# First tokens, first key weights and first key chunks of a gated attention and MLP block, loaded and multiplied in other halves

## The chip, the cores and the metric

The kernel runs on one core of one Trainium2 chip. Its metric is the device time of one execution in microseconds (us), of which several runs are taken and the median is given. The core has a matrix engine (PE, with its weight loads listed as PEld), a vector engine (DVE), an activation engine (ACT), a general engine (POOL) and a synchronising engine (SP), which here issues all DMA transfers. Each engine works through its own list of instructions in order and waits on semaphores for the others.

## The reference

`x` is 2048 tokens of 512 features. Two branches are computed from it and mixed by a gate for each token:

```
g   = sigmoid(sum(x * gate_w))                  # one number for each token
a   = attention(x) @ wo                         # 32 heads of 16, four segments of 512 tokens
b   = (gelu(x @ w_gate) * (x @ w_up)) @ w_down  # 512 -> 1792 -> 512
out = g * a + (1 - g) * b
```

In each segment the attention is causal softmax attention over that segment's 512 tokens. To it is added, by a share for each head, `sigmoid(beta)`, the reading of a memory of the segments before: with phi(t) = t+1 for t>0 and exp(t) otherwise, the memory M sums phi(k) v and z sums phi(k), and the reading is phi(q) M / (phi(q) z). All data is bfloat16, sums are in float32.

## The kernel before, in words

The segments are worked through in order, s = 0 to 3. For a segment, x is kept transposed in `xS[s % 3]`, as 128 features x 4 feature chunks x 512 tokens, so that it can be either operand of a matmul. Keys and queries are made in four chunks of 128 features (eight heads): `u_k(s, c)` (line 364) and `u_q(s, c)` (line 278) each run four matmuls of 128x512 over the feature chunks `fc` into one bank of PSUM, and then `cast` (line 298) copies the bank to bfloat16. For keys two further DVE instructions (line 378) write the chunk twice, with alternate heads zeroed, into `KTm`, which has room for NK = 3 chunks. Values (`u_v`, line 393) take four tiles of 128 tokens.

All these results share one pool, `pgen`, of four PSUM banks, which are handed out in turn by `gen(name)` (line 125). A tile that gets a bank has to wait until the earlier tile in that bank has been read out.

The first stretch is written out by hand; afterwards a planner in Python sets the order of the work from costs and due times. The hand-written part is:

- `load_inputs` (line 134): SP issues, one after the other, two transfers for the first 512 tokens of x, two for wk, then wq, gate_w, wv, beta and w_gate. The two halves of x have 256 tokens each, and partition p gets the two neighbouring tokens 2p and 2p+1 of the half, 2 KB in one piece. The halves of wk are halves of its columns: 256 of the 512 output features, for all input features, in pieces of 512 bytes.
- `warm_up` (line 161): matmuls on constants, whose results are not used.
- `transpose_x0` (line 175): PE transposes these tokens, in four groups of four blocks of 128x128 (token half, and pair of feature chunks). Each group has a bank, which DVE copies to `xS[0]` for the feature chunks 0 and 1, and ACT for 2 and 3. As neighbouring tokens lie in two different blocks, the copies write with a step of two elements.
- `u_k(0, c)` for c = 0, 1, 2 (line 769), `u_q(0, c)` for four chunks, `load_rest` (line 149, further DMA issues), a small transpose of gate_w, four value tiles, the remaining values (`u_vz`), the issue of copies of V, and 14 gate tiles (`u_gate`), which ACT reads out directly.

In this stretch all casts of keys, queries and values go to DVE, since `limit[0]` is still zero. The banks in turn are: warm-up 0 and 1; the four transposed groups 2, 3, 0, 1; key chunks 0 to 2 in 2, 3, 0; query chunks 0 to 3 in 1, 2, 3, 0; gate_w in 1; value tiles 0 to 3 in 2, 3, 0, 1; `u_vz` in 2. So value tile 0 waits for the cast of query chunk 1.

Of the kernel before, what the change touches and what calls it, by code (L numbers as in the profile page):

```python
# [11 lines left out]
ALU = mybir.AluOpType  # L12

P = 128
D = 512
# [4 lines left out]
FC = D // P  # L20
NC8 = H // 8
# [3 lines left out]
NK = 3  # L25
NX = 3
NB = 8
# [9 lines left out]
MM512 = 0.216  # L37
# [16 lines left out]
def kernel(  # L54
# [15 lines left out]
    nc = tc.nc  # L70
# [4 lines left out]
    x2 = A_x[0]  # L75
# [8 lines left out]
    def const(shape, dtype, name):  # L84
        return cpool.tile(shape, dtype, name=name, tag=name)

    xS = [const([P, FC, L], BF, f"x{i}") for i in range(NX)]
    wq = const([P, FC, D], BF, "wq")
    wk = const([P, FC, D], BF, "wk")
# [7 lines left out]
    eo = const([P, 2], F32, "eo")  # L97
# [7 lines left out]
    ktb = const([P, NC8, L], BF, "ktb")  # L105
# [4 lines left out]
    KTm = const([P, NK, NB, 2, 64], BF, "KTm")  # L110
# [14 lines left out]
    def gen(name):  # L125
        return pgen.tile([P, 512], F32, name=name, tag="gen")
# [4 lines left out]
    def cols(dst, src):  # L131
        nc.sync.dma_start(dst[:, :, :], src.rearrange("(fc p) n -> p fc n", p=P))

    def load_inputs():
        half = L // 2
        for i in range(2):
            nc.sync.dma_start(x0[:, 2 * i:2 * i + 2, :],
                              x2[half * i:half * (i + 1), :].rearrange("(p k) d -> p k d", p=P))
        for i in range(2):
            n = slice(D // 2 * i, D // 2 * (i + 1))  # L140
            cols(wk[:, :, n], A_wk[:, n])
        cols(wq, A_wq)
        nc.sync.dma_start(gw4, gate_w.rearrange("(fc p) -> fc p", p=P))
        cols(wv[:, :, 0:D], A_wv)
        nc.sync.dma_start(beta[:, :], A_beta.rearrange("(o n) -> o n", o=1).to_broadcast((P, H)))
        for n in (slice(0, 4 * P), slice(4 * P, DFF)):
            cols(wga[:, :, n], B_w_gate[:, n])
# [27 lines left out]
    def transpose_x0():  # L175
        for half in range(2):
            for f0 in range(0, FC, 2):
                T = pgen.tile([P, 1024], BF, name="x0T", tag="gen")
                for i in range(4):
                    fc, k = f0 + i // 2, i % 2  # L180
                    nc.tensor.transpose(T[:, i * P:(i + 1) * P],
                                        x0[:, 2 * half + k, fc * P:(fc + 1) * P], ident[:, :])
                dst = xS[0][:, f0:f0 + 2, half * 256:half * 256 + 256].rearrange(
                    "q f (p k) -> q f k p", k=2)
                src = T[:, 0:512].rearrange("q (f k p) -> q f k p", f=2, k=2)
                if f0 == 0:
                    nc.vector.tensor_copy(dst, src)
                else:
                    nc.scalar.copy(dst, src)
# [105 lines left out]
    def near(end):  # L295
        return t_act[0] - 1.0 <= end and max(t_act[0], end) + CAST_T <= limit[0]

    def cast(out, src, scale=1.0):
        end = t_pe[0] + MM512
        if near(end):  # L300
            nc.scalar.activation(out, src, AF.Copy, scale=scale)
            t_act[0] = max(t_act[0], end) + CAST_T
            spared[0] = EVAC
        elif isinstance(scale, float):
            nc.vector.tensor_copy(out, src)  # L305
        else:
            nc.vector.tensor_scalar_mul(out, src, scale)
# [7 lines left out]
    general_now = [False]  # L315
# [43 lines left out]
    def u_phk(s, c):  # L359
        def f():  # L360
            phi(ktb[:, c:c + 2, :], ktb[:, c:c + 2, :], ("k", s, c), 1)
        return 0.0, 0.0, f

    def u_k(s, c):
        def f():
            T = gen("kT")
            for fc in range(FC):
                nc.tensor.matmul(T[:, :], lhsT=wk[:, fc, c * P:(c + 1) * P],  # L368
                                 rhs=xS[s % NX][:, fc, :],
                                 start=(fc == 0), stop=(fc == FC - 1))  # L370
                if fc < FC - 1:
                    yield MM512
            cast(ktb[:, c, :], T[:, :])
            if general_now[0]:
                return MM512
            for p in range(2):
                eng = nc.vector if s == 0 and c < NK else nc.gpsimd
                eng.tensor_scalar(out=KTm[:, (NC8 * s + c) % NK, :, p, :],  # L378
                                  in0=ktb[:, c, :].rearrange("q (b k) -> q b k", b=NB),
                                  scalar1=eo[:, p:p + 1], scalar2=None, op0=ALU.mult)  # L380
            return MM512
        return 4 * MM512, EVAC, f

    pk_at = {}

# [226 lines left out]
    def group_qk(pieces):  # L612
        lg = plg.tile([P, 4, 512], F32, name="lg", tag="lg")
        for i, b, off in pieces:
            n = L - 64 * b
            for j in range(4):
                rows = slice(32 * j, 32 * j + 32)
                nc.tensor.matmul(lg[:, j, off:off + n],  # L618
                                 lhsT=KTm[rows, i % NK, b].rearrange("r p k -> r (p k)"),
                                 rhs=QT[rows, i % NC8, 64 * b:L],  # L620
                                 start=True, stop=True, tile_position=(32 * j, 0))
        pT = ptp.tile([P, 4, 512], BF, name="pT", tag="pT")
        nc.scalar.activation(pT[:, :, :], lg[:, :, :], AF.Exp, scale=DH ** -0.5)  # L623
        for _, b, off in pieces:
            for r in range(2):
                v = pT[64 * r:64 * r + 64, :, off:off + 64]
                nc.gpsimd.affine_select(out=v, in_=v, pattern=[[0, 4], [1, 64]],  # L627
                                        compare_op=ALU.is_ge, fill=0.0, base=0,
                                        channel_multiplier=-1)
        return pT  # L630
# [35 lines left out]

    ctx.enter_context(tc.manual_schedule())
    load_inputs()
    make_identity(nc, ident[:, :])
    warm_up()  # L670
    transpose_x0()
    setup_consts()

# [88 lines left out]
    def run(u):  # L762
        if u[0] == 0.0:
            u[2]()
        else:
            for _ in u[2]():
                pass

    for c in range(NK):
        run(u_k(0, c))  # L770
    for c in range(NC8):
        run(u_q(0, c))
    load_rest()
# [34 lines left out]
    for i in range(NK, NSEG * NC8):  # L808
        s, c = i // NC8, i % NC8
        us.append(unit(u_k(s, c), first(i) - 12, ("k", s),  # L810
                       lambda i=i, s=s, c=c: clock[0] >= last(i - NK) and
                       (s == 0 or count(("pk", s - 1)) > c)))
        if c % 2 == 1 and s < NSEG - 1:
            us.append(unit(u_phk(s, c - 1), 0, None,
                           lambda s=s: s == 0 or count(("pk", s - 1)) == NC8))
    streams.append(Stream("K", us))
    us = []
    for i in range(NC8, NSEG * NC8):
        s, c = i // NC8, i % NC8
# [140 lines left out]
    for pieces in visits:  # L960
        clock[0] += 1
        for i, b, off in pieces:
            s, c = i // NC8, i % NC8
# [4 lines left out]
        s = pieces[0][0] // NC8  # L968
        t = group_qk(pieces)
# [8 lines left out]
        if lumps and lumps[0][0] == clock[0]:  # L978
            i = lumps.pop(0)[1]
# [5 lines left out]
        n = len(visits) - clock[0]  # L985
# [80 lines left out]
    def general():  # L1066
# [3 lines left out]
        for s in range(NSEG):  # L1070
# [4 lines left out]
            for c in range(NC8):  # L1075
                run(u_k(s, c))
                run(u_q(s, c))
# [40 lines left out]
            if s < NSEG - 1:  # L1118
# [4 lines left out]
                for half in range(2):  # L1123
# [3 lines left out]
                            scalar1=float(DH ** 0.5 * D * D), scalar2=EXP_LIMIT,  # L1127
                            op0=ALU.mult, op1=ALU.is_le)
# [31 lines left out]
```

## Time and profile before

| what | us |
|---|---|
| median of the runs (lowest, highest) | 270.71 (270.58, 271.08) |
| the profiled execution | 270.57 |
| its span, first to last instruction | 268.8 |
| PE busy in the span | 262.3 |
| ACT busy | 209.0 |
| DVE busy | 203.7 |
| POOL busy | 156.8 |
| first matmul of the keys starts (from the start of the span) | 5.83 |
| first matmul of the queries | 8.50 |
| first matmul of the values | 12.17 |
| first matmul of the gate | 15.69 |

The profile lists instructions with their line in the kernel, engine, tile and duration, and the idle time of the engine ahead of them with what ended it. Matmuls overlap in the records: one of 128x512 is listed with 380 ns, but they start every 216 ns. DVE's records overlap in the same way: the casts of 0.68 us start every 0.60 us. "DMA" as a releaser means that an engine waited for a transfer to land. Times in the profile are from the start of the span, and 1.8 us of the execution lie outside it.

### The profile page before, as it was taken

The numbers are of one execution on the slowest core, as the hardware profiler recorded it, in microseconds if no ns is written. First come the engines' busy times: TensorE is split into PE (matmuls) and PEld (weight loads), VectorE is DVE, ScalarE is ACT, GpSimd is POOL, SyncE is SP. The second block draws the span as 40 slices with busy tenths as digits, with TensorE's granted clock in tenths as the row PEclk, the third lists the DMA queues.
The fourth block names the chain that finished last, engine by engine and source line by source line (L and its number), as shares of the span: only waits on it lengthen the run. The fifth ranks groups of instructions, "written<-read, shape, count | busy, mean of one in ns | idle before, by whom it ended". The sixth has DMA issues, their size and how long they took to land.

```text
span 268.8 us, 6576 instructions
## 1 busy us (share of the span) xinstructions
PE 262.3 (98%) x2713; PEld 117.5 (44%) x2713; DVE 203.7 (76%) x390; ACT 209.0 (78%) x163; POOL 156.8 (58%) x298
## 2 busy tenths in 40 slices
PE   7999999999999999999999999999999999999993
PEld 3454434344453444445444444444444544344441
DVE  2999575868777887697986979596898588697374
ACT  3237889999997998889999988889888987567420
POOL 4000168897905979987811998596875089654400
PEclk9999999999999999999999999999999999999998
DMA  6999901200160000301052002110000200001102
GB/s 205 334 211 321 331 18 35 41 4 0 29 136 2 0 22 22 78 4 41 0 68 56 2 21 50 33 34 8 20 24 21 66 2 20 19 3 41 39 22 85
DMA packets 30282, 16.60 MB, mean 62 GB/s; under 512 B 20008, under 2 KB 28968, under 8 KB 30248
## 3 DMA queue, kind: packets, MB, share of 16 engines
q1 hardware_dynamic: 30248, 16.14, 22.9%
q8 instruction: 22, 0.36, 0.6%
q14 instruction: 12, 0.10, 0.1%
HBM read 8.14 MB, written 2.10 MB: 38 GB/s over the span
## 4 chain that ended last, share of the span: by engine, by line
PE 86%; POOL 5%; issue 4%; DMA 2%; ACT 1%; SPq 0%; DVE 0%; ACTq 0%; DVEq 0%; POOLq 0%
PE gT L456 19%; PE uT L477 17%; PE dT L493 14%; PE lg L618 8%; PE od L643 6%; PE aT L510 5%; PE qT L282 5%; PE kT L368 5%; PE vT L397 4%; POOL pT L627 3%; POOL KTm L378 2%; DMA wk<-in_A_wk_dram 2%; PE MT L531 1%; PE mn L600 1%; ACT pT L623 1%
## 5 line engine op out<-in xcount | busy, mean ns | idle before, releaser
L627 POOL TENSOR_SCALAR_AFFINE_SELECT pT<-pT 64x256 bf16<-64x256 bf16 x256 | 113.8, 445 | 94.2 <-ACT pT L623 81.4
L623 ACT ACTIVATE pT<-lg 128x2048 bf16<-128x2048 f32 x72 | 135.1, 1876 | 24.9 <-PE lg L618 21.6
L477 PE MATMUL uT<-x,wup 128*128 128x512 bf16 x224 | 60.4, 380 | 0.0
L456 PE MATMUL gT<-x,wga 128*128 128x512 bf16 x224 | 57.0, 380 | 0.0
L493 PE MATMUL dT<-wdn,G 128*128 128x512 bf16 x224 | 52.9, 380 | 0.0
L483 DVE TENSOR_TENSOR G<-uT,G 128x512 bf16<-128x512 f32 x56 | 38.1, 684 | 6.4 <-PE uT L477 6.2
L378 POOL TENSOR_SCALAR KTm<-ktb,eo 128x512 bf16<-128x512 bf16 x26 | 40.6, 1572 | 1.3
L650 DVE STREAM_TRANSPOSE oq<-od 128x512 f32<-128x512 f32 x32 | 21.0, 695 | 19.5 <-PE od L643 19.5
L493 PEld LDWEIGHTS <-G 128*128 128x128 bf16 x224 | 20.8, 98 | 25.0 <-issue 2.1
L456 PEld LDWEIGHTS <-wga 128*128 128x128 bf16 x224 | 20.5, 98 | 23.9 <-issue 2.2
L477 PEld LDWEIGHTS <-wup 128*128 128x128 bf16 x224 | 19.8, 97 | 24.0 <-issue 5.4
L618 PE MATMUL lg<-QT,KTm 32*128 32x192 bf16 (+7 forms) x512 | 28.5, 287 | 0.0
L305 DVE CAST G<-gT 128x512 bf16<-128x512 f32 x24 | 16.5, 688 | 9.7 <-PE gT L456 9.5
L618 PEld LDWEIGHTS <-KTm 32*128 32x128 bf16 x512 | 8.3, 92 | 28.4 <-issue 28.1
L643 PE MATMUL od<-pT,V 64*32 64x128 bf16 (+7 forms) x512 | 19.4, 284 | 0.2 <-POOL pT L627 0.2
L643 PE MATMUL od<-pT,Vs 64*32 64x128 bf16 (+7 forms) x512 | 19.4, 284 | 0.0
L471 ACT ACTIVATE G<-G 128x3584 bf16<-128x3584 bf16 x6 | 18.8, 3182 | 0.0
L656 DVE SCALAR_TENSOR_TENSOR o<-oq,ogs,rden 128x256 bf16<-128x256 f32 x32 | 17.0, 532 | 1.1
L368 PE MATMUL kT<-x,wk 128*128 128x512 bf16 x64 | 16.8, 380 | 0.9 <-DMA wk<-in_A_wk_dram 0.9
L282 PE MATMUL qT<-x,wq 128*128 128x512 bf16 x64 | 16.6, 379 | 0.0
L515 DVE SCALAR_TENSOR_TENSOR tB<-aT,gct,tB 128x512 bf16<-128x512 f32 x16 | 11.9, 746 | 6.0 <-PE aT L510 5.7
L510 PE MATMUL aT<-wo,oT 128*128 128x512 bf16 x64 | 16.5, 380 | 0.0
(96 smaller groups left out, 274.8 us busy)
## 6 DMA issues: line engine op xcount, KB each, us to landing
out_dram<-tB SPq DMA_DIRECT2D x16, 128.0 KB, 1.7
wup<-in_B_w_up_dram SPq DMA_DIRECT2D x1, 1792.0 KB, 8.4
wdn<-in_B_w_down_dram SPq DMA_DIRECT2D x1, 1792.0 KB
wga<-in_B_w_gate_dram SPq DMA_DIRECT2D x1, 1280.0 KB, 10.2
Vs<-V SPq DMA_DIRECT2D x8, 144.0 KB, 2.6
G<-in_A_x_dram SPq DMA_DIRECT2D x2, 256.0 KB, 2.8
wk<-in_A_wk_dram SPq DMA_DIRECT2D x2, 256.0 KB, 4.2
wq<-in_A_wq_dram SPq DMA_DIRECT2D x1, 512.0 KB, 5.7
```

The costliest lines, as they stand in the source:

```text
L282: nc.tensor.matmul(T[:, :], lhsT=wq[:, fc, c * P:(c + 1) * P], rhs=xS[s % NX][:, fc, :], start=(fc == 0), stop=(fc == FC - 1))
L368: nc.tensor.matmul(T[:, :], lhsT=wk[:, fc, c * P:(c + 1) * P], rhs=xS[s % NX][:, fc, :], start=(fc == 0), stop=(fc == FC - 1))
L378: eng.tensor_scalar(out=KTm[:, (NC8 * s + c) % NK, :, p, :], in0=ktb[:, c, :].rearrange("q (b k) -> q b k", b=NB), scalar1=eo[:, p:p + 1], ...
L456: nc.tensor.matmul(T[:, :], lhsT=wga[:, fc, hs * P:(hs + 1) * P], rhs=xS[s % NX][:, fc, :], start=(fc == 0), stop=(fc == FC - 1))
L477: nc.tensor.matmul(T[:, :], lhsT=wup[:, fc, hs * P:(hs + 1) * P], rhs=xS[s % NX][:, fc, :], start=(fc == 0), stop=(fc == FC - 1))
L483: nc.vector.tensor_tensor(out=g, in0=T[:, :], in1=g, op=ALU.mult)
L493: nc.tensor.matmul(T[:, :], lhsT=G[s % NG][:, hs, qt * P:(qt + 1) * P], rhs=wdn[:, hs, :], start=(hs == 0), stop=(hs == HS - 1))
L510: nc.tensor.matmul(T[:, :], lhsT=oT[:, fc, qt * P:(qt + 1) * P], rhs=wo[:, fc, :], start=(fc == 0), stop=(fc == FC - 1))
L618: nc.tensor.matmul(lg[:, j, off:off + n], lhsT=KTm[rows, i % NK, b].rearrange("r p k -> r (p k)"), rhs=QT[rows, i % NC8, 64 * b:L], start= ...
L623: nc.scalar.activation(pT[:, :, :], lg[:, :, :], AF.Exp, scale=DH ** -0.5)
L627: nc.gpsimd.affine_select(out=v, in_=v, pattern=[[0, 4], [1, 64]], compare_op=ALU.is_ge, fill=0.0, base=0, channel_multiplier=-1)
L643: nc.tensor.matmul(od[p][32 * j:32 * j + 32, 64 * b:L], lhsT=w[:, 18 * h:18 * h + 32], rhs=t[rows, j, off:off + n], start=(b == 0), stop=( ...
```

## The change

The first 512 tokens still come in two transfers of 256, but partition p now gets tokens p and 128+p of a half ("(k p)" for "(p k)"): two pieces of 1 KB for each partition. The transposed blocks then hold tokens in order, and the copies to `xS[0]` write without a step. The halves of wk are now halves of its rows: the first has the input features of the chunks fc = 0 and 1 for all outputs, in pieces of 1 KB, the second those of fc = 2 and 3. The first three key chunks are no longer made one after the other: three banks are taken at once, the six matmuls with fc = 0 and 1 run for chunks 0, 1, 2, then the six with fc = 2 and 3, and each chunk is cast and masked when its last matmul is done. `u_k`, used for the later chunks, is split into two helpers and issues the same instructions as before.

```diff
-                              x2[half * i:half * (i + 1), :].rearrange("(p k) d -> p k d", p=P))
+                              x2[half * i:half * (i + 1), :].rearrange("(k p) d -> p k d", p=P))
         for i in range(2):
-            n = slice(D // 2 * i, D // 2 * (i + 1))
-            cols(wk[:, :, n], A_wk[:, n])
+            cols(wk[:, 2 * i:2 * i + 2, :], A_wk[D // 2 * i:D // 2 * (i + 1), :])
...
-                dst = xS[0][:, f0:f0 + 2, half * 256:half * 256 + 256].rearrange(
-                    "q f (p k) -> q f k p", k=2)
-                src = T[:, 0:512].rearrange("q (f k p) -> q f k p", f=2, k=2)
+                dst = xS[0][:, f0:f0 + 2, half * 256:half * 256 + 256]
+                src = T[:, 0:512].rearrange("q (f t) -> q f t", f=2)
...
+    def k_part(T, s, c, fcs):
+        for fc in fcs:
+            nc.tensor.matmul(T[:, :], lhsT=wk[:, fc, c * P:(c + 1) * P], rhs=xS[s % NX][:, fc, :],
+                             start=(fc == 0), stop=(fc == FC - 1))
+            if fc < FC - 1:
+                yield MM512
+
+    def k_done(T, s, c):
+        cast(ktb[:, c, :], T[:, :])
+        if general_now[0]:
+            return
+        for p in range(2):
+            eng = nc.vector if s == 0 and c < NK else nc.gpsimd
+            eng.tensor_scalar(out=KTm[:, (NC8 * s + c) % NK, :, p, :],
+                              in0=ktb[:, c, :].rearrange("q (b k) -> q b k", b=NB),
+                              scalar1=eo[:, p:p + 1], scalar2=None, op0=ALU.mult)
+
     def u_k(s, c):
         def f():
             T = gen("kT")
...
+            yield from k_part(T, s, c, range(FC))
+            k_done(T, s, c)
             return MM512
         return 4 * MM512, EVAC, f
+
+    def first_k():
+        Ts = [gen("kT") for c in range(NK)]
+        for c in range(NK):
+            for _ in k_part(Ts[c], 0, c, range(0, FC // 2)):
+                pass
+        for c in range(NK):
+            for _ in k_part(Ts[c], 0, c, range(FC // 2, FC)):
+                pass
+            k_done(Ts[c], 0, c)
...
-    for c in range(NK):
-        run(u_k(0, c))
+    first_k()
     for c in range(NC8):
         run(u_q(0, c))
     load_rest()
```

More of the change, by code (lines that the diff above doesn't have):

```diff
@@ L366, in f @@
             T = gen("kT")
[L367 to L380, printed above, removed]
+            yield from k_part(T, s, c, range(FC))
+            k_done(T, s, c)
             return MM512
         return 4 * MM512, EVAC, f
+    def first_k():
[7 more added lines that the diff above has]
+            k_done(Ts[c], 0, c)
     pk_at = {}
```

## The prediction

> **What bounds the kernel now.** I read the page's busy shares first, then the chain of waits over the first 25 us, then the timeline of the same stretch engine by engine. The page:
>
> ```profile
> PE 262.3 (98%) x2713; PEld 117.5 (44%) x2713; DVE 203.7 (76%) x390; ACT 209.0 (78%) x163; POOL 156.8 (58%) x298
> ```
>
> PE is the bound. The busy times by stretch show it at 10.00 of 10 us from 6 to 16, and also 14.00 of 14, 30.00 of 30 and 60.00 of 60 up to 120 us. So a delay of PE in the first stretch, the only one that is edited, has no later gap to vanish in, and a gain is kept in the same way: what counts is when PE leaves that stretch. The chain of waits there, with start, length and what it is:
>
> ```profile
> 1.71 4.07 DMA wk<-in_A_wk_dram
> 5.78 0.05 issue
> 5.83 2.76 PE kT L368 x12
> 8.59 3.54 PE qT L282 x16
> 12.13 0.11 PE gwT L193
> 12.23 3.13 PE vT L397 x16
> ```
>
> PE waits for the first half of wk until 5.78 and then never again for long. Two things run close beside it, which the timeline shows. First, the inputs of the first matmul, and wq behind it:
>
> ```profile
> 4.28 1.34 DVE L187 COPY x<-x0T 128x512 bf16<-128x512 bf16 x2 [4.28 <-PE x0T L181]
> 4.50 1.32 ACT L189 COPY x<-x0T 128x512 bf16<-128x512 bf16 x2 [2.36 <-PE x0T L181]
> 5.83 2.76 PE L368 MATMUL kT<-x,wk 128*128 128x512 bf16 x12 [0.91 <-DMA wk<-in_A_wk_dram]
> 8.50 1.41 PEld L282 LDWEIGHTS <-wq 128*128 128x128 bf16 x8 [0.40 <-DMA wq<-in_A_wq_dram]
> ```
>
> DVE's second copy ends at 5.62, ACT's at 5.82: the copies end hardly before wk lands. The last key matmul is taken at 8.21 and would free PE at 8.43; the first query matmul starts at 8.50, as wq landed at 8.45. So an earlier start of the keys ends in a longer wait for wq. Second, DVE, which empties the banks:
>
> ```profile
> 6.90 0.69 DVE L305 CAST ktb<-kT 128x512 bf16<-128x512 f32 x1 [1.18 <-PE kT L368]
> 7.63 0.62 DVE L378 TENSOR_SCALAR KTm<-ktb,eo 128x512 bf16<-128x512 bf16 x2
> 8.16 0.69 DVE L305 CAST ktb<-kT 128x512 bf16<-128x512 f32 x1
> 8.88 0.61 DVE L378 TENSOR_SCALAR KTm<-ktb,eo 128x512 bf16<-128x512 bf16 x2
> 9.41 0.68 DVE L305 CAST ktb<-kT 128x512 bf16<-128x512 f32 x1
> 10.13 0.62 DVE L378 TENSOR_SCALAR KTm<-ktb,eo 128x512 bf16<-128x512 bf16 x2
> 10.66 2.48 DVE L305 CAST QT<-qT 128x512 bf16<-128x512 f32 x4
> ```
>
> From 6.90 to 13.14 DVE has no gap: it began when key chunk 0 was done, and is then behind PE, at 1.25 us for a key chunk (PE: 4 x 0.216 = 0.86). The second QT cast starts at 11.26 and ends at 11.94. Its bank is the one that the first value tile takes, at 12.16. So DVE's chain has 0.22 us to spare, 0.18 after a handover of 0.04 (last key matmul's end 6.86 to the cast at 6.90).
>
> **The change part by part.** *The x loads.* By the trace's records of single DMA packets, 2 KB took 85 ns and 1 KB 47 ns, on 16 engines side by side. Each half goes from 8 packets for an engine to 16: 0.75 us for 0.68, so half 0 lands 0.07 later and half 1 0.14 later. They landed at 3.49 and 4.17, now 3.56 and 4.31. PE took half 0 only at 3.76, behind the warm-up matmuls, which are listed up to 3.83; wk and wq were taken 0.04 after they landed. So half 0 costs nothing while it lands before 3.72. Half 1's transposes started at 4.25 and now at 4.35; their first group ended at 4.69, now at 4.79, and DVE can have it at 4.83. DVE's second copy started at 4.91, held by its first copy, so this too is covered. If SP's issue of twice as many pieces takes longer, the bound is its issue rows: 0.41 us for 128 pieces and 0.43 to 0.52 for 512, thus 0 to 0.1; I take 0.02 for each half and still inside the cover.
>
> *The copies.* Four, of 0.73 us each, lose their step of two. The trace has no such copy from PSUM without a step. The nearest rows are the casts from PSUM (0.69, every 0.60) and, at the other end, the KTm writes from SBUF to SBUF (0.35). With the cast's price DVE's copies end at 4.28 + 0.60 + 0.69 = 5.57, with the other at 4.83 + 0.35 = 5.18. I take the cast, which also reads PSUM, and keep both. [...]
>
> *The first half of wk.* Its 16 packets of 1 KB for an engine take 0.75 us where 32 of 512 bytes at 28 ns took 0.90: it gains 0.15 and starts 0.14 later, so it lands as before, at about 5.78. That landing is set by two late engines: the sixteen came in from 4.63 to 5.78, the middle at 4.96, fourteen by 5.30; two packets had stalled for 0.48 and 0.66 us. The next loads show the same lateness over their middle engine: wk's second half 0.50, wq 0.79, wv 0.60, and with this one's 0.82 the mean is 0.68, which puts the landing at 5.64. So the first matmul, 0.05 after it, starts between 5.69 and 5.83; both are later than the copies (5.61 with handover). I take the middle, 5.76. Bounds: 5.22 (copies at 0.35, no late engine) to 6.1 (another 0.3 of lateness).
>
> *The order of the key matmuls.* Still twelve at 0.216. The second half of wk landed at 6.55; it is now wanted at 5.76 + 6 x 0.216 = 7.06 instead of at 7.35, so it is covered. What moves is the end of chunk 0: it came with the fourth matmul, and comes with the eighth, 4 x 0.216 = 0.86 later. Queued behind its cast on DVE are two masks, the other two key chunks, four QT casts, gate_w's copy and the memset that SP waits for ahead of the next x load. Chunks 1 and 2 come every 0.43, so DVE runs without a gap as before, and the whole chain shifts by 0.86 plus the shift of the first matmul: 0.86 - 0.06 = 0.80. The banks of query chunks 1 to 3 are free in time (key chunk 0's cast ends at 6.90 + 0.80 + 0.69 = 8.39 and is wanted at 9.37; chunk 1's at 9.64, wanted 10.24; chunk 2's at 10.89, wanted 11.10). gate_w's bank is free at 12.14, 0.1 late. But the QT cast of chunk 1 ends at 12.74, and value tile 0 is stopped until 12.78 instead of 12.16: **+0.62 us**. After it, value tile 1 needs the bank that is free at 13.34 and comes at 13.54, so nothing is added.
>
> *wq and the SP queue.* Ahead of wq the packets cost 0.27 more in x and 0.26 less in wk (0.14 + 0.14 less 0.15 + 0.15): it lands at about 8.45 as before, and PE, done with keys at 8.36, waits until 8.50. The earlier start of the keys is thus lost there. SP's next x load waits for DVE's memset at 13.09, now some 0.8 later; w_up and the third x load queue behind it, then w_down, wo and the V copies. w_up landed at 24.1 and its first matmul ran at 29.9, the V copies landed at 34.9 and are read at 45.4: 0.8 is covered by both. DVE's reductions end at 26.8 and its next cast is at 29.3. The planner emits the same instructions, so the rest moves as one piece.
>
> **The sum.** 0.86 (DVE's chain) - 0.06 (first matmul) - 0.18 (what the chain had to spare) = 0.62. The profiled execution took 270.57 (span 268.8, and 1.8 around it), so it would take 271.19; the median shown is 0.14 above that execution, so 271.3 as a median.
>
> **The rivals.** *Inputs come in early enough (same).* If the copies are short and wk has no very late engine, the first matmul starts at 5.22 to 5.6 and the bank wait shrinks to 0.08 to 0.46: 270.8 to 271.15. Fourteen of sixteen engines by 5.30 speak for it, the late ones of all four loads against. It becomes the slower case from a first matmul at 5.69 on.
>
> *The copies run at twice the rate (same).* As a mechanism of this kernel: copies that end by 5.2 help only if wk lands before 5.56; with wk at 5.30 the first matmul is at 5.35, the wait 0.20, the time 270.9. It is a half of the case above, 0.17. [...]
>
> *The bank wait never comes (same).* If the banks are not taken in turn, or DVE's chain is quicker than its rows, PE is held only by wq and the time stays at 270.6 to 270.8. Against it: DVE has no gap in its rows, and four banks are four.
>
> *wq comes early (faster).* One mechanism: 1 KB packets let the whole queue run ahead, and wq lands well before 8.45 with PE's keys ready for it. To reach 0.2% (0.54 us, about what a measurement of this kernel can tell from no change) wq has to land by 7.9; the packet prices give 0.0 to 0.1, and the value tile must also be free. At the bound, 270.1.
>
> **How the numbers follow.** The forecast has 0.55: lateness of the loads holds the first matmul at 5.69 or later. The early-input case has 0.34, the missing bank wait 0.07, and faster 0.04. Slower by over 0.2% starts at 271.25, so slower is 0.55, same 0.34 + 0.07 = 0.41, faster 0.04. The range leaves out the missing bank wait and faster (0.11) below and a first matmul after 6.1 (0.05) above: 270.75 to 271.65. The forecast's own part of it is 271.25 to 271.65.
>
> **What would show it.** Right: first key cast near 7.7 instead of 6.90; the second QT cast ending near 12.7; PE idle by some 0.5 us ahead of line 397 with DVE's QT cast named as releaser; first gate matmul near 16.3 for 15.69, and the same distance at the end. Wrong: line 397 with no wait; a first matmul before 5.6; DVE's copies at 0.4 us with PE released by wk at 5.3; wq landing before 8.2; or a wait for x before the transposes that is longer than 0.1, which would add to the time.

## The result and the profile after

The changed kernel is slower: 271.94 us in the median of ten executions (271.44 to 273.76), where the kernel before, timed beside it, has 271.08 (270.58 to 271.39). The ratio is 1.0046, with a 95% interval of 1.0027 to 1.0065. A second comparison gave 1.0046 again (1.0022 to 1.0070). The profiled execution of the changed kernel took 271.95 us, with a span of 270.2.

The chain of waits over the first 30 us of the changed kernel; the columns are start, length and what it is:

```profile
1.81 4.67 DMA wk<-in_A_wk_dram
...
6.52 1.92 PE kT L364 x8
8.44 0.02 issue
8.46 0.70 DVE ktb L303
9.17 0.02 issue
9.19 0.62 DVE KTm L375 x2
9.81 0.61 DVE ktb L303
10.42 0.03 issue
10.44 0.62 DVE KTm L375 x2
11.06 0.61 DVE ktb L303
11.67 0.02 issue
11.69 0.62 DVE KTm L375 x2
12.31 1.21 DVE QT L303 x2
13.52 0.04 issue
13.56 3.19 PE vT L410 x16
```

Before, PE's lines followed one another here. Now the chain leaves PE after eight key matmuls, runs through DVE's casts and masks, and returns to PE only with the value tiles. Rows of the timeline of the same kernel show PE's waits and the shorter copies:

```profile
4.20 0.43 DVE L185 COPY x<-x0T 128x512 bf16<-128x512 bf16 x1 [4.20 <-PE x0T L180]
4.43 1.17 ACT L187 COPY x<-x0T 128x512 bf16<-128x512 bf16 x2 [2.29 <-PE x0T L180]
4.79 0.42 DVE L185 COPY x<-x0T 128x512 bf16<-128x512 bf16 x1 [0.16 <-PE x0T L180]
6.52 2.76 PE L364 MATMUL kT<-x,wk 128*128 128x512 bf16 x12 [1.55 <-DMA wk<-in_A_wk_dram]
12.22 2.48 DVE L303 CAST QT<-qT 128x512 bf16<-128x512 f32 x4
12.96 0.16 PE L191 MATMUL gwT<-ident,G 4*128 4x4 bf16 x1 [0.20 <-DVE QT L303]
13.56 3.19 PE L410 MATMUL vT<-wv,x 128*128 128x448 bf16 x16 [0.44 <-DVE QT L303]
```

Two things are to be read from it. wk's first half landed at 6.48 instead of 5.78, so the keys start at 6.52 instead of 5.83. And value tile 0 starts at 13.56 instead of 12.16, held by DVE's cast of the queries; its distance from the first key matmul grew from 6.34 to 7.04. The first gate matmul comes at 17.07 instead of 15.69, which is 1.38 later, and this is the whole difference of the two profiles (271.95 - 270.57): from that matmul to the end of the span it is 253.15 us in both.

Three of the ten executions took 273.49 to 273.76 us, about 2 us more than the other seven (mean 271.74, against 271.06 for the kernel before). So the mean difference of 1.23 us has two parts: 0.68 in every execution, and 0.55 from three in ten that take 1.85 longer. The experiments look for both.

### The profile page after: what moved, and what is told of

The parts are those of the page before. It is cut to its first block, busy times and chain, and to the rows that moved or that the text cites. A ratio compares the mean times of both kernels' runs of the same rounds, so it can differ in the third digit from the quotient of the medians.

```text
span 270.2 us, 6537 instructions
## 1 busy us (share of the span) xinstructions
PE 258.1 (96%) x2674; PEld 117.5 (44%) x2713; DVE 203.2 (75%) x390; ACT 208.9 (77%) x163; POOL 156.8 (58%) x298
## 4 chain that ended last, share of the span: by engine, by line
PE 81%; POOL 5%; issue 5%; DVE 3%; DMA 2%; ACT 1%; SPq 0%; ACTq 0%; DVEq 0%; POOLq 0%
PE gT L469 18%; PE uT L490 16%; PE dT L506 14%; PE lg L631 8%; PE od L656 6%; PE aT L523 4%; PE vT L410 4%; PE kT L364 4%; PE qT L280 4%; POOL pT L640 3%; POOL KTm L375 2%; DMA wk<-in_A_wk_dram 2%; ACT pT L636 1%; PE MT L544 1%; PE mn L613 1%
## 5 line engine op out<-in xcount | busy, mean ns | idle before, releaser
L490 PE MATMUL uT<-x,wup 128*128 128x512 bf16 x209 | 57.2, 380 | 1.7 <-issue 1.4
L469 PE MATMUL gT<-x,wga 128*128 128x512 bf16 x212 | 55.3, 379 | 1.3 <-issue 1.0
L506 PE MATMUL dT<-wdn,G 128*128 128x512 bf16 x220 | 52.0, 379 | 0.8 <-issue 0.8
L280 PE MATMUL qT<-x,wq 128*128 128x512 bf16 x60 | 15.7, 379 | 0.3 <-DVE tB L528 0.2
L523 PE MATMUL aT<-wo,oT 128*128 128x512 bf16 x61 | 15.8, 380 | 0.1
```

Of the source, the lines that this page charges most:

```text
L280: nc.tensor.matmul(T[:, :], lhsT=wq[:, fc, c * P:(c + 1) * P], rhs=xS[s % NX][:, fc, :], start=(fc == 0), stop=(fc == FC - 1))
L469: nc.tensor.matmul(T[:, :], lhsT=wga[:, fc, hs * P:(hs + 1) * P], rhs=xS[s % NX][:, fc, :], start=(fc == 0), stop=(fc == FC - 1))
L490: nc.tensor.matmul(T[:, :], lhsT=wup[:, fc, hs * P:(hs + 1) * P], rhs=xS[s % NX][:, fc, :], start=(fc == 0), stop=(fc == FC - 1))
L506: nc.tensor.matmul(T[:, :], lhsT=G[s % NG][:, hs, qt * P:(qt + 1) * P], rhs=wdn[:, hs, :], start=(hs == 0), stop=(hs == HS - 1))
L523: nc.tensor.matmul(T[:, :], lhsT=oT[:, fc, qt * P:(qt + 1) * P], rhs=wo[:, fc, :], start=(fc == 0), stop=(fc == FC - 1))
```

## The experiments

Theories of the late wk: A, its layout by rows; B, chance; C, the smaller pieces of x ahead of it. Theory of the order: the interleaved keys delay DVE's chain, and value tile 0 waits for a bank; its rival is that the order costs nothing and the load alone is late. In the diffs the lines with a minus are those of the kernel named.

**The x part alone (kernel before with the x loads and copies of the changed one).**

```diff
-                              x2[half * i:half * (i + 1), :].rearrange("(p k) d -> p k d", p=P))
+                              x2[half * i:half * (i + 1), :].rearrange("(k p) d -> p k d", p=P))
...
-                dst = xS[0][:, f0:f0 + 2, half * 256:half * 256 + 256].rearrange(
-                    "q f (p k) -> q f k p", k=2)
-                src = T[:, 0:512].rearrange("q (f k p) -> q f k p", f=2, k=2)
+                dst = xS[0][:, f0:f0 + 2, half * 256:half * 256 + 256]
+                src = T[:, 0:512].rearrange("q (f t) -> q f t", f=2)
```

> Only the x loads (1 KB pieces) and the copies without a step; wk by columns and the key chunks one after the other, as before. Theory A (the late first half of wk comes from its rows layout, and the lost time is DVE's chain): x halves land near 3.6 and 4.3, copies 0.43 us, wk's first half lands near 5.8 and the first key matmul starts near 5.8; time within 0.2 us of before. Theory B (the lateness is chance, the same for every layout): the same, with the first matmul anywhere from 5.4 to 6.5 and the time up to 0.7 slower where it is late. Theory C (smaller pieces of x make what is queued behind them late): first matmul near 6.5, time +0.6 to +0.8.

Measured: 271.14 us in the median against 270.82, ratio 1.0015 (0.9994 to 1.0035), which is no clear difference. wk's first half landed at 6.42 although it came by columns, and the first key matmul started at 6.46. So theory A falls: the layout by rows is not needed for a late landing. The +0.6 to +0.8 of theory C was not seen either. From there to value tile 0 it took 6.26 us. One execution of eleven took 273.04.

**wk by rows alone (kernel before).**

```diff
-            n = slice(D // 2 * i, D // 2 * (i + 1))
-            cols(wk[:, :, n], A_wk[:, n])
+            cols(wk[:, 2 * i:2 * i + 2, :], A_wk[D // 2 * i:D // 2 * (i + 1), :])
```

> Only wk in halves of rows; x and the order of the key matmuls as before, so that key chunk 0 needs both halves of wk. Theory A: the first half lands near 6.5 and the second near 7.1, so that the third matmul waits until about 7.2, DVE's first cast comes near 7.8 instead of 6.9, the value tile waits for its bank until about 12.9, and the time is +0.75 us. Theory B: halves land near 5.8 and 6.5, first cast 7.0 to 7.2, +0.1 to +0.3 us. Theory C: as B.

Measured: 271.21 against 270.82, ratio 1.0009 (0.9993 to 1.0025). The halves landed at 6.04 and 6.77. The third matmul waited for the second half and started at 6.82, 0.73 after the first, where 0.43 is its pace; so value tile 0 came 6.55 after the first key matmul. Theory A's +0.75 was not seen.

**The order alone (kernel before).**

```diff
-    for c in range(NK):
-        run(u_k(0, c))
+    first_k()
```

> Only the order: the three key chunks interleaved in three banks, with x and wk loaded as before. All theories of the landing: wk's first half lands near 5.8. If DVE's chain of casts and the bank that value tile 0 waits for are what the order costs, the first cast is 0.86 later (7.76), value tile 0 starts at 12.85 instead of 12.16, and the time is +0.68 us. If the order costs nothing and all the loss is the late wk, the time is within 0.1 us of before.

Measured: 271.55 against 270.82, which is +0.73, ratio 1.0028 (1.0011 to 1.0045). The first cast came at 8.05 and value tile 0 at 13.15, 7.10 after the first key matmul at 6.05. The timeline of this kernel, with PE held by the same cast:

```profile
6.05 2.83 PE L366 MATMUL kT<-x,wk 128*128 128x512 bf16 x12 [0.39 <-DVE x L187]
8.05 0.69 DVE L305 CAST ktb<-kT 128x512 bf16<-128x512 f32 x1 [1.96 <-PE kT L366]
13.15 3.19 PE L412 MATMUL vT<-wv,x 128*128 128x448 bf16 x16 [0.44 <-DVE QT L305]
```

The order is the only part of the change whose interval lies clear of 1.

**The changed kernel with the casts of the first keys on ACT.**

In short (the kernel chooses by a flag that `first_k` sets):

```diff
     def k_done(T, s, c):
-        cast(ktb[:, c, :], T[:, :])
+        nc.scalar.copy(ktb[:, c, :], T[:, :])     # for the first three chunks
```

> The changed kernel, with the casts of the first three key chunks on ACT, which is idle there, instead of DVE. DVE's chain then has three casts of 0.60 us less. If the bank wait is real, it goes: value tile 0 starts some 6.25 us after the first key matmul (12.8 for a first matmul at 6.52) instead of 7.03, and the kernel is 0.6 to 0.8 us faster than the changed one, thus +0.3 to +0.6 us of before with wk as late as there. If the loss is all in the late wk, it is as slow as the changed kernel, +1.2 us.

Measured: 271.10 against 270.82, ratio 1.0018 (0.9997 to 1.0039). The keys started at 6.20 and value tile 0 at 12.45. The timeline of this kernel has no wait at the value tiles:

```profile
8.13 1.56 ACT L371 CAST ktb<-kT 128x512 bf16<-128x512 f32 x3 [2.30 <-PE kT L364]
8.75 1.67 DVE L378 TENSOR_SCALAR KTm<-ktb,eo 128x512 bf16<-128x512 bf16 x6 [3.17 <-ACT ktb L371]
12.45 3.20 PE L413 MATMUL vT<-wv,x 128*128 128x448 bf16 x16
```

The distance is 6.26, that of the kernel with the x part alone and the old order. So the interleaving lengthens this distance by 0.78 us (7.036 in the changed kernel, 6.255 here), all of it by the wait for DVE's casts: with these taken off DVE it is gone, although the order stayed. In the timed executions less is gained: without the long ones the mean is 0.27 above that of the kernel before, where the changed kernel is 0.68 above. A reason, argued and not shown, is that the wait for DVE covers other waits of PE: in two profiles of interleaved keys (the changed kernel again, and with filling, both below) PE also waited 0.26 and 0.44 us for wq (counted from 216 ns after the last key matmul had started), and the distance stayed at 7.03 and 7.04. Two of twelve executions still took 272.81 and 272.99; this has another cause.

**The changed kernel and the kernel before once more.**

> The changed kernel once more. Theory B (the landing of wk's first half is chance and the order costs 0.78 us whatever it is): the profiled execution takes 265.46 us plus the start of the first key matmul, value tile 0 starts 7.03 us after that start, and the median is 0.7 to 0.9 us above before. Theory A (rows layout lands late): the first matmul starts at 6.4 or later again, and the median is 1.1 us or more above before.

> The kernel before once more. Theory B: its first half of wk also lands late in most executions, so a profile of it shows the first key matmul at 5.9 to 6.4, and the execution takes 264.7 us plus that start. Theory A: wk by columns lands near 5.8 again, with the first matmul at 5.85 or before.

Measured: the changed kernel 271.72 against 270.89; its keys started at 6.31, value tile 0 came 7.03 later, and the execution took 271.71, where 265.46 + 6.31 is 271.77. Four of twelve took 273.27 to 273.83, the other eight had a mean of 271.59, which is 0.67 above the mean of 270.92 of the kernel before without such executions. The kernel before gave 270.97 (ratio 0.9994, 0.9981 to 1.0007). In its profile wk's first half had landed at 5.24, against theory B, yet its keys started only at 6.04, and the profiled execution took 271.20, where 264.7 + 6.04 would be 270.74. The groups of its transposes and keys (duration in ns: least, median, most) show why:

```profile
L181 PE MATMUL x0T<-ident,G x16: 289/314/314, 3.8 to 5.3; 128*128 128x128 bf16 x16
...
L368 PE MATMUL kT<-x,wk x12: 379/379/591, 6.0 to 8.8; 128*128 128x512 bf16 x12
...
  DVE x L187: 0.4, 1
```

In the profile that the prediction used, the transposes are:

```profile
L181 PE MATMUL x0T<-ident,G x16: 219/219/289, 3.8 to 4.7; 128*128 128x128 bf16 x16
```

The keys of the new profile waited for DVE's copy, because in that execution the transposes started every 107 ns instead of every 56, and the first two keys took up to 591 ns instead of 379. PE was at half its rate until 6.84. In the profile that the prediction used, full rate had come at 3.97.

**wk by rows and the order (x as before).**

> wk by rows and the interleaved order, x loaded and copied as before. Theory B: as the order alone, +0.7 to +0.8 us, with 7.0 us from the first key matmul to value tile 0. Theory A: +1.2 us as the changed kernel. If the new x loads bring anything of their own, this one differs from the changed kernel by it: 1 KB pieces cost 0.14 us of landing, copies with a step cost 0.3 us each, but only where the transposes run at half rate and the copies come after wk.

Measured: 271.64 against 270.89 in the median (271.43 to 271.88), ratio 1.0018 (1.0001 to 1.0034); no execution in twelve was 2 us longer. This is the loss of the order alone; the ratio is lower than the medians because three of the 35 executions of the kernel before took 272.70 to 272.96, and against the mean of the other 32 the difference is 0.74. wk landed at 5.55, the keys started at 6.05 behind the copies, and the full rate of PE came at 6.63, which added 0.25 to the 7.03.

**Filling PE's idle time.** Three matmuls on constants go between the transposes and the first key matmul, into a bank that is not yet in use: first in the kernel with ACT casts, then in the changed kernel itself.

```diff
     def first_k():
+        F = plg.tile([P, 4, 512], F32, name="fill", tag="lg")
+        for i in range(3):
+            nc.tensor.matmul(F[:, 0, :], lhsT=nc.const_aps.tensor(1.0, [P, P], BF),
+                             rhs=nc.const_aps.tensor(1.0, [P, 512], BF), start=True, stop=True)
         Ts = [gen("kT") for c in range(NK)]
```

> The changed kernel with key casts on ACT and three matmuls on constants between the transposes and the first key matmul, so that PE is not idle there. If the executions that take 2 us longer come from PE being at half rate for the first keys after its idle time, they are gone, and the others stay at the time of the kernel with ACT casts (+0.2 us of before), or 0.3 worse where wk comes early. If those come from the loads, one or two executions in ten are still 2 us longer.

> The changed kernel with three matmuls on constants between the transposes and the first key matmul; the casts stay on DVE. Theory H (some executions take 2 us longer because PE is at half rate for the first keys, after too little work before them): no execution near 273.5, all at 271.3 to 272.0, +0.6 to +0.8 us of before. Theory D (these executions come from late loads): three or four in twelve near 273.5 as with the changed kernel.

Measured: with ACT casts 271.18 against 270.89, ratio 0.9998 (0.9981 to 1.0016), the highest of twelve 271.44. The changed kernel with the filling 271.66 against 270.87, ratio 1.0042 (1.0028 to 1.0056), the highest of five 272.48. In neither is an execution near 273, though two of the five, 272.09 and 272.48, lie above the 272.0 that was expected. The distances to value tile 0 stayed at 6.26 and 7.04: the filling leaves the wait for DVE as it is.

**Two more profiles of the changed kernel.**

> The changed kernel, one look. One in three is expected to show an execution of 273.3 to 273.8. Theory H: there the key and query matmuls start every 427 ns instead of 216 until about 10 us, and wk and wq land as in the others. Theory D: matmuls at 216 ns and a load that lands some 2 us later. In a usual execution: first key matmul between 6.0 and 6.6, and 265.46 us more in all.

> The same as the look before it: either an execution near 273.5, which tells half rate of PE (theory H) from a late load (theory D), or the time of 265.46 us plus the start of the first key matmul.

Measured: 271.38 and 273.34. In the second, wk landed at 6.23 and wq at 8.63, no later than in others, but its key matmuls (in the group of the tile kT; least, median, most) are:

```profile
L364 PE MATMUL kT<-x,wk x12: 379/620/634, 6.3 to 10.3; 128*128 128x512 bf16 x12
```

and in the first:

```profile
L364 PE MATMUL kT<-x,wk x12: 379/379/390, 6.0 to 8.3; 128*128 128x512 bf16 x12
```

The chain of waits of the second, where the same eight matmuls that took 1.92 us above take 3.57:

```profile
1.81 4.42 DMA wk<-in_A_wk_dram
6.23 0.05 issue
6.27 3.57 PE kT L364 x8
9.84 0.02 issue
9.87 0.70 DVE ktb L303
```

Single records have the first eight some 427 ns apart, up to 9.66, and 216 after that. Here, too, 253.13 us lie between the first gate matmul and the end. So this longer execution is PE at half rate in its first keys, and theory D, which had put such executions down to a late load, falls for it. It is the only one of them with a profile; that the others are the same is inferred from their length.

**x in large pieces, with copies without a step.**

```diff
-                              x2[half * i:half * (i + 1), :].rearrange("(k p) d -> p k d", p=P))
+                              x2[half * i:half * (i + 1), :].rearrange("(p k) d -> p k d", p=P))
```

> The changed kernel with the first x loaded in pieces of 2 KB as before, while the copies still write without a step; this leaves out the sorting of the first 512 tokens, which end up in another order, so that the output is another one, and the work is the same. Theory C (the smaller pieces of x make wk behind them land late): wk's first half lands at 5.2 to 5.8 instead of 5.9 to 6.5, the first key matmul starts at 5.3 to 5.9, the median is 270.9 to 271.4, and no execution takes 2 us longer. Theory B (chance): the landing at 5.9 to 6.5, the median near 271.7 and two to four executions in twelve near 273.5.

Measured: 271.67 against 270.75, ratio 1.0032 (1.0021 to 1.0044), 271.45 to 271.87 in seven executions. The landing was 6.05 and the keys started at 6.10: theory C's 270.9 to 271.4 was missed, and the usual time is that of the changed kernel. No execution was 2 us longer, which theory B alone had not expected.

**A later wk in the kernel before,** made by a load of 256 KB ahead of it; then the same with five filling matmuls.

```diff
+        cols(wo[:, 0:2, :], A_wo[0:D // 2, :])
         for i in range(2):
             n = slice(D // 2 * i, D // 2 * (i + 1))
```

> The kernel before with 256 KB of wo loaded ahead of wk, which only makes wk land later (by about 0.85 us, 16 packets of 1 KB at 47 ns and their stalls). Theory H2 (a later start of the keys leaves more of the executions at half rate for their first matmuls, whatever made it late): the first key matmul starts at 6.5 to 7.0, the usual execution is 0.5 to 0.9 us longer, and two to five of twelve are 2 us longer again. Theory X (only x in small pieces brings these executions): no more than one in twelve is.

> The same with five matmuls on constants between the transposes and the first key matmul. Theory H2: no execution is 2 us longer than the others, the usual one as without them (0.5 to 0.9 us above before). Theory X: the same; if the longer ones stay, they have nothing to do with PE's idle time.

Measured: the first 272.17 against 270.78, ratio 1.0069 (1.0042 to 1.0095), with three of seven executions at 272.91, 273.72 and 274.02; in the profile the keys started at 6.65. The second 271.65, ratio 1.0036 (1.0023 to 1.0049), 271.44 to 272.09 in five. So x in small pieces is not needed: a later start of the keys is enough for longer executions. With the filling none was seen, which five executions alone would not settle; the counts of all filled kernels are below.

**The starts side by side** (us, from the profiles; the fourth column is the distance from the first key matmul to value tile 0, the last one that from the first gate matmul to the end of the span):

| kernel | wk lands | first key | to value tile 0 | first gate | gate to end |
|---|---|---|---|---|---|
| before, first profile | 5.78 | 5.83 | 6.34 | 15.69 | 253.15 |
| x part alone | 6.42 | 6.46 | 6.26 | 16.24 | 253.20 |
| order alone | 5.65 | 6.05 | 7.10 | 16.66 | 253.15 |
| changed | 6.48 | 6.52 | 7.04 | 17.07 | 253.15 |
| changed, again | 6.26 | 6.31 | 7.03 | 16.84 | 253.13 |
| changed, third profile | 5.91 | 5.96 | 7.03 | 16.50 | 253.15 |
| changed, fourth profile | 6.23 | 6.27 | 8.69 | 18.47 | 253.13 |
| changed, ACT casts | 6.15 | 6.20 | 6.26 | 15.97 | 253.15 |

## Why the prediction was right and wrong

The range ended at 271.65, and the measured median is 271.94. The mechanism held. What failed is the term for the first key matmul, which stood on wk landing as before, together with the base that was drawn from the same early profile; and the sum had no term for executions whose first keys run at half rate. Each is taken up below.

**Right: the direction and its mechanism.** The bank of value tile 0 waits for the cast of query chunk 1, which DVE reaches late, since key chunk 0 ends with the eighth matmul. The prediction's 5.76 for the first key and 12.78 for value tile 0 are 7.02 us apart; the five profiles of interleaved keys at full rate whose copies came before wk have 7.03 to 7.04. The experiments with the order alone and with ACT casts show it from both sides. That all behind it moves as one piece was right to 0.1 us, and the sum of +0.62 is close to the 0.67 and 0.68 by which the usual executions differ. That it is so close is partly luck: the order lengthened the distance by 0.78 and not by 0.68, and in the profile after the keys started 0.69 later and not 0.06 earlier, so that the two profiles differ by 1.38.

**Right: the x loads.** Half 0 and half 1 were put at 3.56 and 4.31 and landed at 3.58 and 4.30; the transposes of half 1 were put at 4.35 and started at 4.35. SP's issue of them took longer than the 0.02 for each half that was assumed: 0.47 and 0.45 us for 0.40 and 0.41, so that wk was issued at 1.81 instead of 1.71.

**Wrong without weight: the copies.** The sum took 0.69 us, the price of a cast; they take 0.43 on DVE and 0.59 on ACT. For DVE the other row that the prediction kept, 0.35, was the nearer one. The shorter copies gained nothing in the changed kernel's profile, where the copies ended at 5.21 and 5.60 and wk landed at 6.48.

**Wrong: "so it lands as before, at about 5.78".** The first half of wk landed at 6.48 in the profile after, six of its sixteen DMA engines later than 5.6 (two in the profile before), the middle one at 4.89 (4.96 before). The sum had -0.06 for the first matmul, and this profile had +0.69. A start after 6.1 was given a chance of 0.05, yet the four profiles of the changed kernel have 5.96, 6.27, 6.31 and 6.52. In eight profiles with x in pieces of 1 KB the last engine came in at 5.91 to 6.48 (mean 6.20), in the six with 2 KB and no load added at 5.24 to 6.05 (mean 5.72). The last engines overlap, and the kernel with 2 KB pieces and short copies came in at 6.05 with a usual time that was no better. The engines that were later than 5.6 do not overlap: four to nine of sixteen in each of the eight profiles, none to three in each of the six. So the traces speak for theory C, in the landing though not in the time; what in the pieces holds these engines back stays open. That it hardly shows in the timed means fits three profiles with 2 KB pieces in which the transposes ran at half rate (a step of 107 ns in the second profile of the kernel before) and the slower copies (0.73 us for 0.43 on DVE) held the keys until 6.04 or 6.05; this is argued.

**Wrong: the base.** The 271.3 was set on a median of three runs, 270.71, and on a profile with an early wk and PE at full rate from 3.97. The ten runs that these three belong to have 271.08, and the kernel's second profile started the keys at 6.04; six later sets of 9 to 35 executions have medians of 270.75 to 270.97. Of the 0.64 us between 271.3 and 271.94, this base is 0.37. Nearly all of the rest is what the three long executions do to the median: that of the other seven is 271.68. Also, 0.07 of the 0.18 us that DVE's chain was said to have to spare was PE's wait for wq in that profile; with 0.11 to spare the order would cost 0.75, near the 0.78 of the distances.

**Missed: PE at half rate for the first keys.** No rival had it. In the execution of 273.34 us their step was 427 ns instead of 216. With x in 1 KB pieces and no filling, 11 of 47 timed executions were about 2 us longer; the kernel before had 4 of 124, the four other kernels with x in 2 KB pieces and no load added none of 41, and the three kernels with filling none of 22. The delayed wk brought three of seven without x in small pieces. Why the changed kernel has more of them than the order alone, whose usual time is the same, follows only in part: its keys started at 5.96 to 6.52 in four profiles, those of the unfilled kernels with 2 KB pieces and no load added at 5.83 to 6.10, and the end of the half rate falls anywhere from 3.8 to 6.8. PE's idle time alone does not decide it: in the changed kernel's second profile (271.71 us) the transposes also ran at half rate, PE then stood idle for 0.64 us, and the keys started at 6.31 at full rate; in the execution of 273.34 us it was 0.62 us, and the keys started at 6.27 at half rate. That the later start alone makes the share of long executions is argued from this and from the delayed wk, not shown for the changed kernel.

The rivals: early inputs did not come about. The missing bank wait and an early wq were refuted by the 0.44 us wait and by wq's landing at 9.09, 0.6 later than before. None of the kernels tried beats the one before: the nearest, ACT casts with filling, is at 0.9998 (0.9981 to 1.0016), and 0.21 us above the mean of the kernel before without its three long executions.

## What to carry to other kernels

If results are interleaved so that they finish later and closer together, follow the engine that empties them: its whole queue moves by the delay of the first result, and the loss comes up at the next bank it owes, not at the edit. Counted from the first key matmul, the first cast here started at 1.94 us for 1.08, the second cast of the queries ended at 6.98 for 6.12, and value tile 0 started at 7.04 for 6.34. Before a sum is set on a profile of a start-up, see how its landings and rates vary: in such a stretch one profile is one draw (the kernel before started its keys at 5.83 in one profile and at 6.04 in another). And where PE idles shortly after its start, look at whether its first matmuls run at half rate (427 ns a step for 216 in the execution of 273.34 us); work that nobody needs can be cheaper than the gap. Here no long execution was seen in 22 with such work, and the mean of all executions was 271.12 with it and 271.36 without it under ACT casts, 271.89 (five executions) and 272.25 to 272.30 in the changed kernel.

## What the runs showed of the hardware

PE's step for a 128x512 matmul was 427 ns (the first keys of the execution of 273.34 us) or 216 ns, and for the transposes 107 (the second profile of the kernel before) or 56 (its first). The time from which it ran at the full rate was 3.8 to 6.8 us in fifteen of the sixteen profiles, though all had the same warm-up from 0.97 on; in the execution of 273.34 us it was 9.66, and the granted clock of its profile stands at 1.00 in that stretch too:

```profile
6.00:7.00 1.00, 0.73 (x2) 0.28 (x3) 0.00 (x0) 0.28 (x1) 0.00 (x0) 1.00 1.03 337
7.00:8.00 1.00, 1.00 (x4) 0.35 (x3) 0.00 (x0) 0.00 (x0) 0.00 (x0) 1.00 0.80 256
```

These are busy times by stretch (length; PE, weight loads, DVE, ACT, POOL with counts; clock; DMA): four matmuls are at work between 7 and 8 us, and three start there (7.10, 7.53, 7.95), at a clock of 1.00, so the half rate has to be read from the matmuls themselves. The starts of the full rate that can be seen in the other profiles lie between 3.97 and 6.84; in the execution of 273.34 us PE stood idle from 5.66 to 6.27 before it. What decides when the full rate comes is not shown by these runs.

A DVE copy of 128x512 from PSUM took 0.71 to 0.73 us with a step of two elements in its output (kernel before) and 0.43 without (changed kernel); an ACT copy took 0.73 and 0.59.
